# Quarter-array projections of a two-branch attention kernel: roundings, subtractions, no-operations and query loads placed by the planner, low parts written over their copies

## The chip, the cores and the metric

The kernel runs on one core of one Trainium2 chip. The metric is the device time of one execution in microseconds (us); the time given for a kernel is the median of several runs. A profiled execution adds a trace of what every engine did.

## The reference

Two attention blocks over the same input `x` (2048 rows of 448), each with its own weights, are mixed by a gate per row:

```
g = sigmoid((x * gate_w).sum(-1, keepdims=True))
a = A_ref(x, A_wqkv, A_wo)     # 16 heads of 28; each row attends to itself and 7 earlier rows, 2 apart
b = B_ref(x, B_wqkv, B_wo)     # 16 heads of 28; full softmax attention over all 2048 rows
return g * a + (1 - g) * b
```

Both blocks project `x` by a 448x1344 matrix to queries, keys and values and end with a 448x448 output product. All data is 32 bits wide.

## The kernel before, in words

**Two parts for one number.** A 32-bit operand is held as a rounded high part (type float32r) and a low part, the difference between the number and its high part. A product is the sum of three: high by high, high by low, low by high.

**Stages.** The kernel has (1) the first eleven projection tiles, which use all 128 rows of the TensorE array; (2) the quarter-array projections, which the change touches; (3) the attention of block B, 16 units of 16 steps, with block A's work on VectorE and GpSimd beside it; (4) the output products.

**Stage 2.** It makes tiles 11 to 90 of the list `tiles`: 17 tiles of queries and keys of B (512 columns), 16 of values of B and 47 of the 48 for A (448 columns; the last is made later by `last_tile`). Here every matmul uses 32 rows of the array, a quarter, and four run side by side. The function `quarters` (L391) writes the order of the matmuls out in advance. It keeps a planned time for TensorE, VectorE and ScalarE and for each of the eight PSUM banks, takes the matmul that can start first, and appends it to `plan`. A tile takes up to 42 quarter matmuls, all into one bank, first one quarter's share, then the next one's (`TURN`). Between two quarters of one tile stands a no-operation on GpSimd or ScalarE (L363): it waits for the last matmul of the one quarter, and the first of the other waits for it (the code's reason is "other rows, same bank"). An instruction on a queue waits for those ahead of it, a no-operation too.

**Score maxima.** Block B subtracts from its scores the maximum of each row. The maxima of the first 320 of 1024 score blocks are computed in stage 2, between the projections: `s1_quarter` (L169) issues one matmul of keys by queries (L152; one of four heads, so also a quarter of the array) into a free bank and one VectorE reduction of 512 columns out of it (L172). Sixty-four of them are a unit. `AHEAD` (L389) limits how many matmuls one head may be ahead of the one furthest behind. The queries of a unit lie in a pair of tiles, `QP[u % 2]`, so unit 2 uses the pair of unit 0. `load_qhi(u + 1)` (L150) is called when the first matmul of unit u is issued.

**Around a tile.** When the last matmul of a query or key tile is done, `qk_tile` (L464) copies the bank to SBUF on ScalarE (`raw`, L472), rounds the copy to the high part on ScalarE (`qkh`, L473) right behind it, has GpSimd subtract (L256) after 32 further product matmuls, and stores both parts to HBM after 43 (SP queue, L461). The three results take three half tiles of the pool `pp`, which has 16. Value and A tiles are only copied (L478). The weights of the next tiles are rounded on ScalarE (L324) and subtracted on GpSimd (L256). The maxima of a finished unit are gathered by `max_parts` (L182): a small VectorE reduction, two ScalarE instructions and one GpSimd subtraction (L193).

After stage 2 all eight banks are given back, and the attention begins with new PSUM tiles (`T`, `av`).

Of the kernel before, what the change touches and what calls it, by code (L numbers as in the profile page):

```python
# [21 lines left out]
NU = NG * NB  # L22
# [4 lines left out]
def gated_mix_kernel(ctx: ExitStack, tc: tile.TileContext, xT, xn, gw, wA, wB, woAB, out):  # L27
# [116 lines left out]
    def s1_mm(n, bank):  # L144
# [4 lines left out]
        if i == 0 and u + 1 < NU:  # L149
            load_qhi(u + 1)  # L150
        r = slice(32 * h, 32 * h + ROWS)
        nc.tensor.matmul(bank, qhis[u][h % 2][r, 128 * qs:128 * qs + 128],  # L152
                         KH[u // NB % 3][r, 512 * kc:512 * kc + 512], start=True, stop=True)
# [14 lines left out]

    def s1_quarter(h, bank):  # L169
        n = 4 * count[h] + h  # L170
        s1_mm(n, bank)
        nc.vector.tensor_reduce(MX[:, n % NMX:n % NMX + 1], bank, axis=X, op=ALU.max)  # L172
# [56 lines left out]
    if True:  # L229
# [10 lines left out]
        queue, sent = [], [0]  # L240
        clock = [0.0, 0.0, 0.0]

        def pool_op(cost, f):
            clock[1] = max(clock[1], clock[0]) + cost
            f()

        def soon(k, f):
            queue.append((sent[0] + k, f))
            queue.sort(key=lambda x: x[0])

        def run_queue():
            while queue and queue[0][0] <= sent[0]:
                queue.pop(0)[1]()

        def low_part(lo, raw, hi):
            soon(32, lambda: pool_op(0.3 + 0.002 * lo.shape[-1], lambda: nc.gpsimd.tensor_tensor(  # L256
                out=lo, in0=raw, in1=hi.bitcast(F32), op=ALU.subtract)))


        def both(dst, src, eng=nc.sync):  # L260
            for h in (0, 64):
# [53 lines left out]
        def split_w(wi, kts):  # L315
            if wi not in wsets:
                wsets[wi] = ([KL[0][:, 512 * i:512 * i + 512].rearrange("p (k c) -> p k c", k=4) for i in range(2)]
                             if wi == 2 else
                             [wp.tile([128, 4, 450], F32R, tag=g, name=f"{g}{wi}") for g in ("wh", "wl")])
            wh, wl = wsets[wi]  # L320
            r, t, n = wraw[wi]
            for kt in kts:
                raw = r[:, kt, :n] if kt < 3 else t[:, :n]
                nc.scalar.activation(wh[:, kt, :n], raw, AF.Copy)  # L324
                if wi > 1:
                    low_part(wl[:, kt, :n], raw, wh[:, kt, :n])
                else:
                    nc.gpsimd.tensor_tensor(out=wl[:, kt, :n], in0=raw, in1=wh[:, kt, :n].bitcast(F32), op=ALU.subtract)

# [6 lines left out]
                 for n in range(2)]  # L336

        SECOND = [(0, 0, 3), (0, 1, 3), (0, 0, 0), (0, 1, 0), (0, 0, 1), (0, 1, 1), (1, 0, 0), (0, 0, 2), (0, 1, 2),
                  (1, 0, 1), (1, 0, 2)]

        def product(n, p, q, bank, first, last, leaves=False):
            t = tiles[n]
            ws = wsets[t[0]]
            rows = slice(0, 128) if q is None else slice(32 * q, 32 * q + 32)
            a, c, k = p
            if t[1] == "qk":
                x = (xh[t[2]], xl[t[2]])[a][rows, k, :]
                i = nc.tensor.matmul(bank, ws[c][rows, k, t[4]:t[4] + 128], x, start=first, stop=last)  # L348
            else:
                j = t[-1]  # L350
                cols = D + 2 * (t[0] == GATE)
                x = (xh[j // 4], xl[j // 4])[a][rows, k, 128 * (j % 4):128 * (j % 4) + 128]
                i = nc.tensor.matmul(bank[:, 0:cols], x, ws[c][rows, k, 0:cols], start=first, stop=last)  # L353
            if q is not None:
                if n in moved:
                    follows(i, moved.pop(n))
                if leaves:
                    at_ = clock[0] + REACH
                    if max(clock[1], at_) <= max(clock[2], at_) + WORD:
                        eng, clock[1] = nc.gpsimd, max(clock[1], at_) + WORD  # L360
                    else:
                        eng = nc.scalar
                    moved[n] = eng.nop()  # L363
                    follows(moved[n], i)

        moved = {}
# [19 lines left out]

        TURN = ((0, 4, 3, 2, 1), (1, 0, 4, 3, 2), (2, 1, 0, 4, 3), (3, 2, 1, 0, 4))
        LOAD, REACH, SUM, NOP, WORD = 0.107, 0.43, 0.598, 0.16, 0.05
        HUNGER, AHEAD = 0.1, 2  # L389

        def quarters(n0, n1, maxima):  # L391
            todo = [[n for k in range(n0, n1, 5) for n in (k + i for i in TURN[q]) if n < n1] for q in range(4)]
# [6 lines left out]
            plan = []  # L399
            while any(todo) or any(stay):  # L400
                b = min(range(8), key=lambda i: free[i])

# [4 lines left out]
                for q in range(4):  # L407
# [11 lines left out]
                    if p[0] < 1e8 and (best is None or p < best):  # L419
                        best = p  # L420
                t, product_, q, wait = best
                issue, now_, begun[q] = max(issue, wait) + 0.003, t, t
                if not product_:
                    sent[q] += 1
                    end[q] = t + 0.2315
                    dve = max(dve, t + REACH) + SUM
                    free[b] = dve + 0.092 + WORD
                    plan.append((t, act, "max", q, b))
                    continue
                if not stay[q]:  # L430
                    n = todo[q].pop(0)
# [12 lines left out]
                plan.append((t, act, "product", n, p, q, home[n], first, last, leaves and not last))  # L444
# [6 lines left out]
            return plan  # L451


        fini = []
# [1 line left out]
        def qk_store(nb, rows, hi, lo):  # L456
            cs = slice(512 * nb, 512 * nb + 512)
            for dst, t in ((qk_hi, hi), (qk_lo, lo)):
                o = 0
                for r0, r1 in rows:  # L460
                    dma_r(dst[r0:r1, cs], t[o:o + r1 - r0])  # L461
                    o += r1 - r0

        def qk_tile(n, bank, now_, nb, rows):  # L464
            hi, lo = ptile("qkh").bitcast(F32R), ptile("qkl").bitcast(F32R)
            if n < FULL:
                nc.scalar.activation(hi, bank, AF.Copy)
# [3 lines left out]
            raw = ptile("raw")  # L471
            nc.scalar.activation(raw, bank, AF.Copy)  # L472
            nc.scalar.activation(hi, raw, AF.Copy)  # L473
            low_part(lo, raw, hi)
            soon(43, lambda: qk_store(nb, rows, hi, lo))

        def copy_tile(bank, dst):
            nc.scalar.activation(dst, bank[:, 0:D].rearrange("p (c e) -> p c e", e=dst.shape[-1]), AF.Copy)  # L478

        stage = {}  # L480

        def a_tile(n, bank, i, j):
            k = i, j // 2
            s = stage.get(k)
            if s is None:
                stage[k] = pair("ast").rearrange("p a b -> p (a b)")[:, 0:896].rearrange("p (c j e) -> p c j e", c=8, j=2)
            copy_tile(bank, stage[k][:, :, j % 2, :])
            if tiles[n][0] == GATE:
                nc.scalar.activation(zt[:, j:j + 1], bank[:, D:D + 1], AF.Copy)
            if s is not None:  # L490
                j -= j % 2
                nc.sync.dma_start(a_own[i][:, :, j:j + 2, :].rearrange("c p j e -> p c j e"), stage.pop(k))
# [93 lines left out]
        def behind(n):  # L586
# [12 lines left out]
                load_w(1, (True,))  # L599
            if n == 40:  # L600
                for i in range(4):
                    soon(20 * i, lambda i=i: init_kl(KL[0][:, 512 * i:512 * i + 512]))
            if n == 16:
                for i in (1, 2):
                    nc.sync.dma_start(a_scr[i][:, 0:NJ, :].rearrange("c j e -> c (j e)").rearrange(
                        "c (a b) -> c a b", b=NJ), omg[0:8, None, :].to_broadcast([8, 56, NJ]))
            if n == 32:
                for i in range(2):
                    soon(20 * i, lambda i=i: nc.gpsimd.memset(V[:, 8 * i:8 * i + 8, :, DH:], 1.0))
            if n == 22:  # L610
                load_k(1, KH[1], qk_hi)
            if n == 62:
# [7 lines left out]
            if n == 64:  # L620
                for sgn, dst in ((-1.0, g_t), (1.0, omg)):
                    e = sp.tile([128, NJ], F32, name="ez")
                    nc.scalar.activation(e, zt, AF.Exp, scale=sgn)
                    nc.gpsimd.tensor_tensor(out=e, in0=e, in1=V[:, 0, :, DH], op=ALU.add)
                    gate.append((dst, e))
            if n in (66, 68):
# [18 lines left out]
            behind(n)  # L645
        n = FULL
        before(n)
        for clock[0], clock[2], kind, *x in quarters(FULL, len(tiles) - 1, MAXIMA):
            if kind == "max":
                s1_quarter(x[0], PS[x[1]])  # L650
                continue
            product(*x[:3], PS[x[3]], *x[4:])
            sent[0] += 1
            run_queue()
# [6 lines left out]
        assert not queue  # L661

# [592 lines left out]
```

## Time and profile before

| | |
|---|---|
| median of 3 runs | 896.5 us (896.09 to 896.72) |
| the profiled execution's own time | 896.25 us |
| its span, first to last instruction | 894.5 us |
| quarter-array projections in it | about 36 to 249.4 us |
| attention and output products | 249.4 to 894.5 us |
| busy over the span: TensorE, VectorE, ScalarE, GpSimd | 881.3, 746.8, 610.1, 544.5 us |
| mean granted TensorE clock | 0.998 of full speed |

In the profile, PE is TensorE's matmuls and PEld its weight loads (each matmul has one), DVE is VectorE, ACT ScalarE, POOL GpSimd, SP the queue that issues DMAs. A "q" behind an engine (ACTq) means the queue's own instructions, such as the no-operations. "Idle before" is the time in which the engine did nothing before an instruction, and the name behind the arrow is what ended it. Matmuls overlap here, so PE counts as busy even when only one of four quarters works. Times are from the span's start.

### The profile page before, as it was taken

To read this page: it belongs to the slowest core of one execution; us is meant where nothing else is said; L and a number is where in the kernel's file an instruction comes from. 1 tells how busy PE (TensorE), PEld (TensorE's weight loads), DVE (VectorE), ACT (ScalarE), POOL (GpSimd) and SP (SyncE) were. 2 spreads that over 40 slices of the span, in tenths; PEclk is the share of its full clock that TensorE was granted. 3 is DMA by queue.
4 is the path that set the end of the run, shared out by engine and by line. 5 is a ranking of instruction groups with operands and counts; after the bars stand their busy time and mean duration, and the time that the engine had idled before them with its cause. 6 is when DMAs were issued, how large, how long until landed. Compare 5 with 4: busy or idle time off the path is not lost.

```text
span 894.5 us, 24181 instructions
## 1 busy us (share of the span) xinstructions
PE 881.3 (99%) x9988; PEld 525.9 (59%) x9988; DVE 746.8 (83%) x1128; ACT 610.1 (68%) x780; POOL 544.5 (61%) x413
## 2 busy tenths in 40 slices
PE   9997999999999999999999999999999999999998
PEld 7886999999954444444444444444444444434997
DVE  7685999999989999999999999999999999832221
ACT  6253223231178898898988989989889898897220
POOL 1164311020059689998989989999999799701000
PEclk9999999999999999999999999999999999999999
DMA  9868503445392251225225322433121321337691
GB/s 263 265 220 232 171 14 97 117 115 136 85 289 67 84 141 49 65 63 156 71 57 141 87 58 89 126 92 105 47 60 31 92 44 46 106 82 209 174 284 52
DMA packets 114199, 104.76 MB, mean 117 GB/s; under 512 B 75256, under 2 KB 82424, under 8 KB 113304
## 3 DMA queue, kind: packets, MB, share of 16 engines
q1 hardware_dynamic: 113656, 102.42, 41.0%
q8 instruction: 78, 1.28, 0.6%
q10 hardware_dynamic: 432, 0.79, 0.3%
q14 instruction: 33, 0.27, 0.1%
HBM read 62.20 MB, written 40.96 MB: 115 GB/s over the span
## 4 chain that ended last, share of the span: by engine, by line
PE 89%; DVE 1%; DMA 1%; ACT 0%; issue 0%; SPq 0%; POOLq 0%; ACTq 0%
PE T L1157 31%; PE av L1123 28%; PE r L353 14%; PE T L991 8%; PE T L152 4%; PE r L152 2%; PE r L348 2%; DVE MX L172 1%; DMA QP<-qk_hi 1%; PE av L553 0%; ACT P L1162 0%; SPq L104 0%; ACT onhi L1048 0%; ACT raw L472 0%; DVE res L1112 0%
## 5 line engine op out<-in xcount | busy, mean ns | idle before, releaser
L1162 ACT ACTIVATE P<-T 128x1024 f32<-128x1024 f32 x512 | 496.7, 1023 | 59.2 <-PE T L1157 57.4
L158 DVE TENSOR_REDUCE MX<-T 128x1 f32<-128x512 f32 x470 | 442.2, 954 | 31.7 <-PE T L152 20.2
L1123 PE MATMUL av<-P,V 128*32 128x512 f32 x2048 | 272.7, 605 | 0.0
L1157 PEld LDWEIGHTS T<-QH,KH 30*128 30x128 f32 x1024 | 92.3, 181 | 230.0 <-ACT P L1162 196.5
L152 PE MATMUL T<-KH,QP 30*128 30x512 f32 x704 | 220.9, 458 | 0.0
L1157 PE MATMUL T<-QH,KH 30*128 30x512 f32 x1024 | 211.9, 489 | 1.1 <-DVE MX L172 0.9
L172 DVE TENSOR_REDUCE MX<-r 128x1 f32<-128x512 f32 x320 | 197.1, 683 | 15.8 <-PE r L152 11.4
L1157 PE MATMUL T<-QH,KL 30*128 30x512 f32 x1024 | 185.5, 393 | 0.0
L1157 PE MATMUL T<-QL,KH 30*128 30x512 f32 x1024 | 183.2, 388 | 0.0
L353 PE MATMUL r<-wh,xh 32*128 32x448 f32 (+1 forms) x1008 | 150.8, 368 | 0.7 <-POOLq L363 0.7
L353 PE MATMUL r<-wl,xh 32*128 32x448 f32 (+1 forms) x882 | 144.4, 364 | 0.0
L758 POOL TENSOR_TENSOR prod<-qt,kt 128x896 f32<-128x896 f32 x64 | 135.5, 2118 | 3.3 <-DMA kt<-a_scr 3.3
L353 PE MATMUL r<-wh,xl 32*128 32x448 f32 (+1 forms) x756 | 136.3, 364 | 0.0
L353 PEld LDWEIGHTS r<-wh,xh 32*128 32x128 f32 x1008 | 125.6, 184 | 2.3 <-POOLq L363 1.5
L152 PE MATMUL r<-KH,QP 30*128 30x512 f32 x320 | 120.6, 404 | 5.4 <-DMA QP<-qk_hi 5.3
L353 PEld LDWEIGHTS r<-wl,xh 32*128 32x128 f32 x882 | 119.2, 185 | 0.1
L353 PEld LDWEIGHTS r<-wh,xl 32*128 32x128 f32 x756 | 107.0, 185 | 0.1
L819 POOL TENSOR_TENSOR oat<-oat,prod 128x896 f32<-128x896 f32 x48 | 101.3, 2110 | 2.0
L152 PEld LDWEIGHTS T<-KH,QP 30*128 30x128 f32 x704 | 86.0, 181 | 25.6 <-ACT P L1162 15.4
L814 POOL TENSOR_TENSOR prod<-vt,L 128x896 f32<-128x896 f32 x56 | 95.4, 1704 | 0.3
L1157 PEld LDWEIGHTS T<-QL,KH 30*128 30x128 f32 x1024 | 94.0, 184 | 0.0
L1157 PEld LDWEIGHTS T<-QH,KL 30*128 30x128 f32 x1024 | 92.9, 182 | 0.2
(134 smaller groups left out, 1057.8 us busy)
## 6 DMA issues: line engine op xcount, KB each, us to landing
a_scr<-ast SPq DMA_DIRECT2D x24, 448.0 KB
qk_hi<-qkh SPq DMA_DIRECT2D x24, 256.0 KB
qk_lo<-qkh SPq DMA_DIRECT2D x24, 256.0 KB
rbc<-rs SPq DMA_DIRECT2D x64, 64.0 KB
QP<-qk_hi SPq DMA_DIRECT2D x64, 56.0 KB
KL<-qk_lo SPq DMA_DIRECT2D x16, 224.0 KB
QH<-qk_hi SPq DMA_DIRECT2D x64, 56.0 KB
QL<-qk_lo SPq DMA_DIRECT2D x64, 56.0 KB
```

The costliest lines, as they stand in the source:

```text
L152: nc.tensor.matmul(bank, qhis[u][h % 2][r, 128 * qs:128 * qs + 128], KH[u // NB % 3][r, 512 * kc:512 * kc + 512], start=True, stop=True)
L158: i = nc.vector.tensor_reduce(MX[:, n % NMX:n % NMX + k], bank, axis=X, op=ALU.max)
L172: nc.vector.tensor_reduce(MX[:, n % NMX:n % NMX + 1], bank, axis=X, op=ALU.max)
L348: i = nc.tensor.matmul(bank, ws[c][rows, k, t[4]:t[4] + 128], x, start=first, stop=last)
L353: i = nc.tensor.matmul(bank[:, 0:cols], x, ws[c][rows, k, 0:cols], start=first, stop=last)
L758: nc.gpsimd.tensor_tensor(out=p, in0=qt[c], in1=kvt["k", c % 2][:, HALO - DIL * w:HALO - DIL * w + NJ, :], op=ALU.mult)
L814: nc.gpsimd.tensor_tensor(out=dst.rearrange("p j (h d) -> p j h d", d=DH), in0=kvt["v", c % 2][:, HALO - DIL * w:HALO - DIL * w + NJ, :].r ...
L819: nc.gpsimd.tensor_tensor(out=ows[c % 2][:, :, 0:56] if w == W - 1 else oat[c], in0=oat[c], in1=oat[c, w], op=ALU.add)
L991: writes(bank, nc.tensor.matmul(bank[:, cols], src, wo[c][k][:, cols], start=(first and k == ks[0] and i == 0), stop=(last and k == ks[-1] ...
L1123: nc.tensor.matmul(av[32 * h:32 * h + 32, :], V[:, kt, 4 * g + h, :], tiles_[h], start=(kt == 0), stop=(kt == NJ - 1), skip_group_check=True)
L1157: nc.tensor.matmul(bank[a], (KH[g % 3], KH[g % 3], KL[g % 2])[t][r, ks], (qh, ql, qh)[t][r, :], start=(t == 0), stop=(t == 2))
L1162: e = nc.scalar.activation(p, one if a == "2" else mine, AF.Exp, scale=SCALE).ins
```

## The change

- **Query loads.** `load_qhi(u + 1)` is no longer called at the first matmul of unit u, but when all four heads have issued their 64 of the unit before; the very first matmul still loads unit 1. `AHEAD` goes from 2 to 1.
- **Roundings.** The high part of a query or key tile is no longer rounded right behind its copy. The planner puts a "round" into the plan at the first time at which it sees ScalarE free, and plans the copy alone (0.607 in place of 1.214) ahead of the release of the bank.
- **Low parts.** The subtraction writes over the copy (`lo = raw`), so that a tile takes two half tiles and not three. Subtractions (of weights too) are taken from a list of jobs when they fit before the next no-operation; where a whole one does not fit, it is split into two halves of the columns. The stores follow the second half.
- **No-operations.** GpSimd or ScalarE is chosen by planned times of both, which now count the copies, roundings and subtractions that were placed.
- **Memsets and gate.** The memsets of `V` and `KL` and the gate's two additions go through the same list; the gate's two reciprocals come one tile later each.

```diff
     def s1_quarter(h, bank):
         n = 4 * count[h] + h
-        s1_mm(n, bank)
+        if n == 0:
+            load_qhi(1)
+        s1_mm(n, bank, True)
...
             if done % 64 == 0:
                 finished.append(done // 64 - 1)
+                if done < MAXIMA:
+                    load_qhi(done // 64 + 1)
...
+        def soon(delay, f, pool=(), patience=4.0):
+            jobs.append((clock["now"] + delay, clock["now"] + delay + patience, pool, f))
+            jobs.sort(key=lambda x: x[0])
...
+                if pool:
+                    begin = max(clock["pool"], t)
+                    room = turns[0] + 0.3 - begin if turns else 9.0
+                    fit = [c for c in pool if c <= room] or [c for c in pool[-1:] if t >= late]
+                    if begin > t + 0.1 or not fit:
+                        continue
...
+        def low_part(lo, raw, hi, delay, then=None):
...
+                nc.gpsimd.tensor_tensor(out=lo[:, p], in0=raw[:, p], in1=hi[:, p].bitcast(F32), op=ALU.subtract)
...
+            soon(delay, part, (1.28, 0.75))
...
-        HUNGER, AHEAD = 0.1, 2
+        HUNGER, AHEAD = 0.1, 1
...
+                if round_ and max(act, round_[0][0]) <= t:
+                    act = max(act, round_[0][0]) + 0.64
+                    plan.append((t, "round", round_.pop(0)[1]))
...
-                    act += 1.214 if cols[n] == 512 else 0.553
+                    act += 0.607 if cols[n] == 512 else 0.553
+                    if cols[n] == 512:
+                        round_.append((act + 0.1, n))
...
+        def qk_round(n):
+            _, _, nb, rows, _ = tiles[n]
+            hi, raw = ptile("qkh").bitcast(F32R), raws_.pop(n)
+            lo = raw.bitcast(F32R)
+            nc.scalar.activation(hi, raw, AF.Copy)
...
+            low_part(lo, raw, hi, 0.75, lambda: soon(0.9, lambda: qk_store(nb, rows, hi, lo)))
```

Three places show how the order moves. First, TensorE at the change from unit 0 to unit 1 of the maxima. The rows are matmuls, output<-inputs; L152 is a maximum's matmul, QP00 and QP01 hold the queries of unit 0 and later of unit 2, QP10 and QP11 those of unit 1. Before:

```order
L348 MATMUL r4_144<-xl1_208,KL0_169 128x512
L353 MATMUL r6_152<-wl3_927,xh0_203 128x448 [waits Pool_49]
L152 MATMUL r3_140<-KH0_167,QP01_174 128x512 [waits DMAHW2_49,Activation_49]
L348 MATMUL r5_148<-xl3_210,KL0_169 128x512
L353 MATMUL r2_136<-wh3_926,xh0_203 128x448 [waits DVE_49]
L353 MATMUL r6_152<-wh3_926,xl0_207 128x448
L353 MATMUL r0_128<-wl3_927,xh2_205 128x448
```

Now:

```order
L390 MATMUL r4_144<-wh3_908,xh0_203 128x448
L385 MATMUL r1_132<-xh3_206,KL0_169 128x512
L385 MATMUL r3_140<-xl2_209,KL0_169 128x512
L385 MATMUL r6_152<-xh1_204,KL0_169 128x512
L152 MATMUL r2_136<-KH0_167,QP00_173 128x512 [waits DVE_49]
```

In both, one head issues its last matmul of unit 0 after the others have begun unit 1. Before, the load of unit 2 into the same tile stood ahead of it in the program, so it waits for that load (DMAHW2); now the load stands behind it, and it waits for a bank alone.

Second, ScalarE at the second group of query and key tiles: a row from a bank (r0 to r7) is a copy, a row from `raw` or `qkr` a rounding. Before:

```order
L472 ACTIVATE raw_812<-r2_136 128x512
L473 ACTIVATE qkh_1061<-raw_812 128x512
L472 ACTIVATE raw_1079<-r7_156 128x512
L473 ACTIVATE qkh_1078<-raw_1079 128x512
L472 ACTIVATE raw_1079<-r1_132 128x512
L473 ACTIVATE qkh_1088<-raw_1079 128x512
L472 ACTIVATE raw_1102<-r6_152 128x512
```

Now:

```order
L522 ACTIVATE qkr_1044<-r5_148 128x512
L522 ACTIVATE qkr_1044<-r0_128 128x512
L522 ACTIVATE qkr_1086<-r1_132 128x512
L352 ACTIVATE wh3_908<-wt_606 128x448
L522 ACTIVATE qkr_1086<-r3_140 128x512
L522 ACTIVATE qkr_1103<-r2_136 128x512
L510 ACTIVATE qkr_1103<-qkr_1044 128x512
L510 ACTIVATE qkh_1163<-qkr_1044 128x512
```

Before, each copy waited behind the rounding of the tile ahead of it; now five copies stand ahead of the first rounding.

Third, GpSimd at the same place: subtractions of `qk` tiles and of the weights `wl`. Before:

```order
L256 TENSOR_TENSOR wl3_927<-raw_610,wh3_926 128x448 x3
L256 TENSOR_TENSOR qkh_1061<-raw_812,qkh_1061 128x512
L256 TENSOR_TENSOR qkh_1078<-raw_1079,qkh_1078 128x512
L256 TENSOR_TENSOR qkh_1088<-raw_1079,qkh_1088 128x512
L256 TENSOR_TENSOR qkh_1101<-raw_1102,qkh_1101 128x512
```

Now:

```order
L280 TENSOR_TENSOR wl3_909<-raw_605,wh3_908 128x448
L280 TENSOR_TENSOR qkr_785<-qkr_785,qkh_854 128x256 x2
L280 TENSOR_TENSOR wl3_909<-raw_605,wh3_908 128x224
L280 TENSOR_TENSOR wl3_909<-wt_606,wh3_908 128x224
L280 TENSOR_TENSOR wl3_909<-raw_605,wh3_908 128x224
L280 TENSOR_TENSOR qkr_1044<-qkr_1044,qkr_1103 128x256
```

Whole subtractions in a row have become halves, and halves of weights and of tiles alternate. The no-operations are not listed in these rows. Counted in the two programs, 198 stood on GpSimd and 42 on ScalarE before, 210 and 30 now; 15 of GpSimd's stood right behind a subtraction before, 34 now; and stage 2 has 37 subtractions before and 63 now. The 320 maxima and the quarter matmuls of the products are the same in number.

More of the change, by code (lines that the diff above doesn't have):

```diff
@@ L148, in s1_mm @@
             qs, kc = i // 8 % 4, 2 * (i // 32) + i // 4 % 2
-        if i == 0 and u + 1 < NU:
+        if i == 0 and not early and u + 1 < NU:
             load_qhi(u + 1)
@@ L238, in split @@
             nc.vector.tensor_tensor(out=lo, in0=raw, in1=hi.bitcast(F32), op=ALU.subtract)
[L240 to L257, printed above, removed]
+        jobs, sent, turns = [], [0], []
@@ new lines, in gated_mix_kernel, with run_jobs @@
+        clock = {"now": 0.0, "pool": 0.0, "act": 0.0}
+        def soon(delay, f, pool=(), patience=4.0):
+            jobs.append((clock["now"] + delay, clock["now"] + delay + patience, pool, f))
+            jobs.sort(key=lambda x: x[0])
+        def run_jobs(t):
+            clock["now"] = t
+            while turns and turns[0] < t:
+                turns.pop(0)
+            for j in list(jobs):
+                ready, late, pool, f = j
+                if ready > t:
+                    break
+                if pool:
[4 more added lines that the diff above has]
+                        continue
+                    clock["pool"] = begin + fit[0]
+                    jobs.remove(j)
+                    f(fit[0])
+                    continue
+                jobs.remove(j)
+                f()
@@ new lines, in act_busy, with part @@
+        def act_busy(cost, ready=0.0):
+            clock["act"] = max(clock["act"], clock["now"], ready) + cost
+        def low_part(lo, raw, hi, delay, then=None):
+            n = lo.shape[-1]
+            def part(c, begin=0):
+                p = slice(begin, n if c > 1 or begin else n // 2)
+                nc.gpsimd.tensor_tensor(out=lo[:, p], in0=raw[:, p], in1=hi[:, p].bitcast(F32), op=ALU.subtract)
+                if p.stop < n:
+                    soon(0.0, lambda c: part(c, p.stop), (0.75,), 2.0)
+                elif then:
+                    then()
+            soon(delay, part, (1.28, 0.75))
@@ L357, in product @@
                 if leaves:
[L358 to L363, printed above, removed]
+                    then = clock["now"] + REACH
+                    key = min(("pool", "act"), key=lambda k: max(clock[k], then) + WORD * (k == "act"))
+                    clock[key] = max(clock[key], then) + WORD
+                    moved[n] = (nc.gpsimd if key == "pool" else nc.scalar).nop()
                     follows(moved[n], i)
@@ L443, in quarters @@
                 last, leaves = not left[n], not stay[q]
-                plan.append((t, act, "product", n, p, q, home[n], first, last, leaves and not last))
+                plan.append((t, "product", n, p, q, home[n], first, last, leaves and not last))
                 if leaves:
@@ L470, in qk_tile @@
                 return
[L471 to L475, printed above, removed]
+            raws_[n] = ptile("qkr")
+            nc.scalar.activation(raws_[n], bank, AF.Copy)
+            act_busy(0.607, clock["now"] + REACH)
         def copy_tile(bank, dst):
             nc.scalar.activation(dst, bank[:, 0:D].rearrange("p (c e) -> p c e", e=dst.shape[-1]), AF.Copy)
+            act_busy(0.553, clock["now"] + REACH)
         stage = {}
@@ L647, in gated_mix_kernel @@
         before(n)
-        for clock[0], clock[2], kind, *x in quarters(FULL, len(tiles) - 1, MAXIMA):
+        plan = quarters(FULL, len(tiles) - 1, MAXIMA)
+        turns.extend(x[0] + REACH for x in plan if x[1] == "product" and x[8])
+        for t, kind, *x in plan:
+            run_jobs(t)
             if kind == "max":
@@ L660, in gated_mix_kernel @@
                 before(n)
-        assert not queue
+        assert not jobs
     hooks = {}
```

33 lines of the change are left out of this document (22 added, 11 removed).

## The prediction

> **What bounds the kernel now.** I read the mean times by stretch first: one row for the first part of the quarter-array stage, which holds nearly all its query and key tiles, one for the rest. Columns: stretch, length, busy time and count of PE, PEld, DVE, ACT and POOL, granted TensorE clock, DMA share, GB/s.
>
> ```profile
> 36.00:100.00 64.00, 56.73 (x904) 52.05 (x900) 50.41 (x83) 21.86 (x43) 25.09 (x24) 0.97 0.75 225
> 100.00:250.00 150.00, 148.41 (x2769) 145.56 (x2765) 147.09 (x249) 40.85 (x102) 20.02 (x25) 1.00 0.38 101
> ```
>
> From 100 us on TensorE and VectorE are both full (2765 weight loads in 150 us, 18.4 per us). Before 100 us both have holes: 52.05 of 64 us of weight loads, 50.41 of 64 us on VectorE. What the change can bring lies there. Next the waits of the weight loads from 36 to 250 us, since matmuls overlap and a weight load shows when the issue stands still (columns: total us, times, longest):
>
> ```profile
> PEld r L152 <- issue: 5.7, 1, 5.7
> PEld r L348 <- ACTq L363: 3.0, 3, 1.6
> PEld r L353 <- POOLq L363: 1.5, 2, 1.1
> PEld T L1157 <- DVE MX L172: 1.2, 1, 1.2
> PEld r L152 <- DVE MX L172: 0.8, 3, 0.3
> PEld r L348 <- POOLq L363: 0.3, 1, 0.3
> ```
>
> Together 12.5 us. The first is one stop of 5.7 us, the next three of ScalarE's no-operations. TensorE's timeline places them (start, length, row, idle time before it and what ended it):
>
> ```profile
> 53.61 0.50 PE L348 MATMUL r<-xh,wh 32*128 32x512 f32 x1 [0.70 <-ACTq L363]
> ...
> 69.17 0.49 PE L348 MATMUL r<-xh,wh 32*128 32x512 f32 x1 [1.21 <-ACTq L363]
> ...
> 87.16 0.76 PE L152 MATMUL r<-KH,QP 30*128 30x512 f32 x1 [5.33 <-DMA QP<-qk_hi]
> ...
> 173.06 0.47 PE L353 MATMUL r<-wh,xh 32*128 32x448 f32 x1 [0.72 <-POOLq L363]
> ```
>
> The long one is a maximum's matmul that waits for queries to land. VectorE's waits in the stage are the other side of these holes, 15.1 us in all:
>
> ```profile
> DVE MX L172 <- PE r L152: 11.4, 10, 6.6
> DVE MX L172 <- PE r L348: 2.5, 2, 2.3
> DVE MX L172 <- PE r L353: 1.2, 1, 1.2
> ```
>
> From 237.27 us to the stage's end the chain of work lies on VectorE (20 reductions), so it bounds the stage as closely as TensorE does:
>
> ```profile
> 237.27 12.12 DVE MX L172 x20
> ```
>
> **The change part by part.** *Query loads.* The SP queue issues the four loads of unit 2 here, and the clock's rows after the stop follow (stretch, PE busy, granted clock, DMA share, GB/s):
>
> ```profile
> 81.24 1.61 SPq L104 DMA_DIRECT2D QP<-qk_hi  x4
> ```
>
> ```profile
> 86.00:87.00 1.00, 0.00 (x0) 0.90 1.00 328
> 87.00:88.00 1.00, 0.84 (x8) 0.50 0.77 199
> 88.00:89.00 1.00, 1.00 (x14) 0.50 0.89 203
> 89.00:90.00 1.00, 1.00 (x18) 0.50 0.88 213
> 90.00:91.00 1.00, 1.00 (x23) 0.89 0.41 94
> ```
>
> The loads were issued when unit 1 began, and head 3 still had its last matmul of unit 0 to issue, out of a tile that one of them writes. It waited until they had landed, and all four quarters stood behind it. Now the load is issued after that matmul, and unit 2 is needed 64 maxima later, some 39 us at 0.61 us each (12.12 / 20). So the 5.7 us go whole. The clock at half speed behind the stop goes with them: 0.84 us of work and two whole rows at half, and a tenth of a row, 0.42 + 0.5 + 0.5 + 0.11, some 1.5 us. The Trainium skill (TensorE: Matmul & The Clock Gate, "What's actually happening") says that the clock drops to half after an idle window of about 3.4 us, for at least one such window; the rows agree. By its figure a whole window would have cost 1.7 us, and the sum below would be 0.2 us lower.
>
> SP now waits for the unit's last matmul before it issues the loads, and stores of the next tiles are queued behind it. I cost that at nothing: the half tiles those stores free are needed only after several more tiles. Without that cover it would cost one such group of issues, 1.6 us. A lower `AHEAD` gives the planner fewer choices for a maximum's head; since from the 64th on the maxima stand some 20 to 40 products earlier in TensorE's order than before (counted in the two orders), I cost it at nothing too.
>
> *Roundings.* ScalarE's share in the stage:
>
> ```profile
> L473 ACT ACTIVATE qkh<-raw 128x512 fp32r<-128x512 f32 x17 | 10.7, 632 | 0.9
> L472 ACT ACTIVATE raw<-r 128x512 f32<-128x512 f32 x17 | 9.9, 585 | 15.8 <-PE r L348 9.4 <-PE r L152 6.4
> ```
>
> The tiles come in groups of about five. Five pairs are 5 x 1.22 us, 6.1 us in one piece, and the no-operations at 53.61 and 69.17 us stood behind such pieces; the copies, which free banks, were spaced by roundings. Now five copies take 2.9 us, and the roundings follow. The two ACTq waits that the timeline shows go. The third, too short to show there, is of a no-operation behind the gathering of unit 0's maxima, which keeps its form; of the 3.0 us I leave 0.3 for it. So 2.7 us. What is late next at those places is a bank, held by VectorE, and that is work, no hole.
>
> *Subtractions and half tiles.* GpSimd's rows, by form:
>
> ```profile
> L256 POOL TENSOR_TENSOR qkh<-raw,qkh 128x512 fp32r<-128x512 f32 x17 | 21.4, 1287 | 15.6 <-ACT qkh L473 7.9 <-DMA qk_hi<-qkh 7.7
> L256 POOL TENSOR_TENSOR wl<-raw,wh 128x448 fp32r<-128x448 f32 x9 | 10.4, 1158 | 31.3 <-PE r L152 15.9 <-PE r L353 14.2 <-ACT wh L324 1.2
> L256 POOL TENSOR_TENSOR KL<-raw,KL 128x128 fp32r<-128x128 f32 x3 | 1.3, 446 | 13.0 <-PE r L348 13.0
> ```
>
> A half of 256 columns I estimate between the first and the last row: 446 + (1287 - 446) / 3 is 726 ns, so each split adds some 165 ns to GpSimd, 26 splits 4.3 us. GpSimd is busy 25 of the first 64 us; that is hidden as long as no no-operation waits behind it. The 7.7 us for a store to free a half tile go, since a tile takes two of 16 now; TensorE waited for none of it, so I count nothing.
>
> *No-operations.* One stood behind a gathering at 173 us:
>
> ```profile
> 173.02 0.22 POOL L193 TENSOR_TENSOR nmt<-nmv,nmt 128x16 fp32r<-128x16 f32 x1 [20.88 <-ACT nmv L192]
> ```
>
> The gatherings stay as they are, so I leave the POOLq waits of this kind in. Right behind a subtraction stood 15 of GpSimd's before, and 34 stand there now. The price is bounded by two rows: all 15 behind whole subtractions together cost at most the 0.3 us of the POOLq wait at L348 (the 1.5 us at L353 belong to another kind, no-operations behind a gathering's subtraction, below), so 19 more would cost 0.4 us; at the other end each waits for a whole half, 19 x 0.73, 13.9 us. Below nothing: the better choice of queue could also take the 1.8 us of POOLq waits. I take 0.9 us, near the row that shows the same thing.
>
> *The rest.* Memsets, the gate's additions and reciprocals are small, and their results are read in the attention, 40 us and more later; nothing. The attention and what follows (249.4 to 894.5 us) keep their order and 704 maxima, and move as one piece.
>
> The sum: 5.7 + 1.5 + 2.7 - 0.9 is 9.0 us off the profiled execution's own 896.25 us, 887.25 us. The median of the runs shown is 0.25 us higher, so I forecast 887.5 us. VectorE allows it, having 15.1 us of holes.
>
> **The rivals.** *Draining the banks is the bound (faster still).* If TensorE's smaller waits for banks, under 0.25 us and in no row above, vanish too because copies come earlier, the stage shrinks until VectorE's holes are gone: at most 15.1 us, or 12.2 if the 2.9 us remain that it is not busy after 100 us (150 - 147.09). That is 884.3 us, with 881.4 as the end. For it speaks the chain's end on VectorE; against it, that 18.4 weight loads per us are already reached between 100 and 250 us, and the sum of TensorE's holes is smaller. The Trainium skill (TensorEngine Tiling (Array Packing), "PSUM Bottleneck") has the rule that tiling speeds up the array but not the emptying of PSUM, which may become the bottleneck. The trace agrees in part: both are full.
>
> *Half of it comes back.* The plan is made of planned times; where a copy or rounding runs later than planned, subtractions and no-operations behind it do too. If each of the three groups of tiles keeps one hole of the size seen (1.2 or 1.6 us), or the gatherings cost 1.1 us four times in place of once, 3.3 (3 x 1.1) to 4.8 us (3 x 1.6) return: 890.8 to 892.3 us.
>
> *No-operations behind halves (slower).* Place: GpSimd's queue during the query and key tiles and at each weight set. If the 19 added ones wait 0.73 us each, 13.9 us against 9.9 gained: 4 us slower, 900.5 us. It turns slower at 0.52 us each. Against it speaks the 0.3 us for 15.
>
> *The change doesn't do what it says.* If another matmul still waits for a load, or a bank held by VectorE stands where the stop was, only the ScalarE part remains: 2.7 - 0.9, 894.7 us. Against it: the only late matmul of unit 0 now waits for a bank alone.
>
> **How the numbers follow.** Forecast 0.62 (its own range 885.5 to 890), the faster rival 0.12, half of it back 0.15, no-operations slower 0.06, the change without its main part 0.05. The range 883.5 to 893.5 us leaves out the slower rival, the last one and the tail of the faster. A difference of 0.2%, 1.8 us, is what a measurement of this kernel can tell from none. Faster: 0.62 + 0.12 + 0.15 less the forecast's own risk of a hole that I don't see, 0.87; within 0.2%: 0.05, mostly the change without its main part; slower: 0.08, the no-operations and that unseen hole.
>
> **What would show it.** Right: no wait of PE or PEld for a DMA of QP between 36 and 250 us; the clock at 1.00 in every row there; ACTq waits under 0.6 us; VectorE's waits down to 3 to 6 us; its last reduction out of a bank r at about 240 us; 645 us from there to the end, as before. Wrong: POOLq waits above 5 us in total (no-operations), a DMA in front of L152 (queries) or of a copy (half tiles), or clearly fewer weight loads between 36 and 100 us than the 17.3 per busy us of now (900 / 52.05) without any named wait, which would put the loss on banks.

## The result, and the profile after

| | before | after |
|---|---|---|
| median of 4 runs | 896.61 us (896.09 to 896.86) | 883.37 us (883.11 to 883.54) |
| ratio, 95% interval | | 0.9853 (0.9836 to 0.987) |
| the profiled execution's own time, its span | 896.25, 894.5 us | 883.11, 881.3 us |
| quarter-array projections end at | 249.4 us | 236.3 us |
| attention and output products | 645.1 us | 645.0 us |

The change makes the kernel 13.2 us faster. All of it comes out of the quarter-array stage, which ends 13.1 us earlier. The forecast was 887.5 us, a gain of 9.0 us, with 883.5 us as the low end, so the direction was right and the size too small.

The mean times by stretch of the kernel after, with the columns as before; the second stretch ends at 237 us now, just behind the end of the stage:

```profile
36.00:100.00 64.00, 64.00 (x1109) 62.51 (x1109) 63.19 (x105) 25.23 (x51) 34.00 (x49) 1.00 0.75 226
100.00:237.00 137.00, 136.72 (x2560) 133.75 (x2556) 134.96 (x228) 36.65 (x93) 15.47 (x27) 1.00 0.41 109
```

The first stretch, which was the one with holes, is full: 1109 weight loads where there were 900, VectorE busy 63.19 of 64 us where it was 50.41, the clock at 1.00. The second stretch has the density it had. The waits of the weight loads from 36 to 238 us:

```profile
PEld r L152 <- DVE MX L174: 0.7, 3, 0.3
PEld T L1212 <- ACT ast L526: 0.7, 1, 0.7
PEld r L390 <- ACT zt L538: 0.5, 2, 0.3
PEld r L390 <- POOLq L398: 0.4, 1, 0.4
PEld av L603 <- issue: 0.4, 1, 0.4
PEld r L385 <- DVE MX L174: 0.3, 1, 0.3
```

Together 3.0 us, where there were 12.5. The query stop is gone, no ACTq wait is left, and POOLq is down from 1.8 to 0.4 us. VectorE's waits in the same stretch, which were 15.1 us:

```profile
DVE MX L158 <- PE T L152: 1.2, 1, 1.2
DVE MX L174 <- PE r L152: 0.8, 3, 0.4
```

The end of the stage in the chain of waits (start, length, what):

```profile
232.39 1.04 PE r L390 x16
233.43 0.17 PE r L152
233.61 0.61 PE r L390 x11
...
234.25 0.66 PE r L390 x10
...
235.74 0.55 ACT ast L526
236.29 0.04 issue
236.33 0.50 PE T L1212 x2
```

Before, the last 12 us of the stage hung on VectorE's reductions; now its end hangs on TensorE's product matmuls and the last copy. From 36 to 237 us the rows above leave VectorE idle for 2.9 of 201 us and the weight loads for 4.7, so little is left to gain in this stage by moving work about.

### The profile page after: what moved, and what is told of

Same layout as the page of the kernel before. It is cut to its first block, busy times and chain, and to the rows that moved or that the text cites. A ratio compares the mean times of both kernels' runs of the same rounds, so it can differ in the third digit from the quotient of the medians.

```text
span 881.3 us, 24193 instructions
## 1 busy us (share of the span) xinstructions
PE 876.9 (100%) x9988; PEld 524.6 (60%) x9988; DVE 747.3 (85%) x1128; ACT 609.3 (69%) x780; POOL 549.1 (62%) x439
## 4 chain that ended last, share of the span: by engine, by line
PE 99%; ACT 0%; issue 0%; DVE 0%; ACTq 0%
PE T L1212 31%; PE av L1178 29%; PE r L390 15%; PE r L385 8%; PE T L1046 8%; PE T L152 4%; PE r L152 3%; PE r L227 1%; PE av L603 0%; ACT P L1217 0%; ACT ast L526 0%; ACT onhi L1103 0%; DVE res L1167 0%; ACT L L839 0%; ACTq L1103 0%
## 5 line engine op out<-in xcount | busy, mean ns | idle before, releaser
L152 PE MATMUL T<-KH,QP 30*128 30x512 f32 x704 | 220.7, 458 | 0.0
L390 PE MATMUL r<-wl,xh 32*128 32x448 f32 (+1 forms) x882 | 146.6, 363 | 0.0
L390 PE MATMUL r<-wh,xl 32*128 32x448 f32 (+1 forms) x756 | 139.8, 362 | 0.0
L390 PEld LDWEIGHTS r<-wh,xh 32*128 32x128 f32 x1008 | 129.9, 184 | 1.3 <-ACT zt L538 0.5
L152 PE MATMUL r<-KH,QP 30*128 30x512 f32 x320 | 123.3, 400 | 0.0
L390 PEld LDWEIGHTS r<-wl,xh 32*128 32x128 f32 x882 | 121.0, 184 | 0.1
L390 PEld LDWEIGHTS r<-wh,xl 32*128 32x128 f32 x756 | 110.9, 184 | 0.1
L152 PEld LDWEIGHTS T<-KH,QP 30*128 30x128 f32 x704 | 86.0, 181 | 25.9 <-ACT P L1217 16.3
```

## The experiments

Four theories stand in the expectations. **S**: the gain is a sum of the stops that the trace of before names (query load, no-operations on ScalarE and GpSimd). **V**: it ends where VectorE has no holes left. **B**: what the sum lacks are small waits for banks whose copies stand behind roundings. **P**: it is TensorE's new order. Unless said otherwise a kernel keeps the order of TensorE's instructions of the kernel that it is made from. The kernel before ran beside each: its median was 897.03, 896.94 and 897.02 us in the three groups, 0.4 us above that of the table, so differences under half a microsecond between groups are not told apart.

**The late query load alone, on the kernel before.**

```diff
-    def s1_mm(n, bank):
+    def s1_mm(n, bank, early=False):
...
-        if i == 0 and u + 1 < NU:
+        if i == 0 and not early and u + 1 < NU:
             load_qhi(u + 1)
...
-        s1_mm(n, bank)
+        if n == 0:
+            load_qhi(1)
+        s1_mm(n, bank, True)
...
             if done % 64 == 0:
                 finished.append(done // 64 - 1)
+                if done < MAXIMA:
+                    load_qhi(done // 64 + 1)
```

> The kernel before with one part of the change: the queries of unit u+1 are loaded when all four heads have issued the last matmul of unit u-1's tile pair, not at unit u's first matmul; the order of TensorE is that of before. Theory S (each named stop is a term of its own): 5.7 us of stop and 1.5 us of half clock go, 7.2 us in all, 889.4 us. Theory V (VectorE bounds the stage, so a stop of TensorE costs only what VectorE was starved): its 6.63 + 1.21 us of idle there go, 888.8 us. If the stop was covered by the VectorE queue at the stage's end, less than 4 us: over 892.5 us.

Measured: 890.08 us (889.85 to 890.28), ratio 0.992 (0.9905 to 0.9935), 6.95 us less than before. The waits of its weight loads from 36 to 236 us:

```profile
PEld r L352 <- ACTq L367: 4.1, 4, 1.6
PEld r L357 <- POOLq L367: 1.4, 2, 1.1
PEld r L152 <- DVE MX L174: 0.6, 2, 0.3
PEld r L352 <- POOLq L367: 0.3, 1, 0.3
```

and TensorE's timeline at the three largest of the first row:

```profile
53.64 0.50 PE L352 MATMUL r<-xh,wh 32*128 32x512 f32 x1 [0.70 <-ACTq L367]
...
69.20 0.49 PE L352 MATMUL r<-xh,wh 32*128 32x512 f32 x1 [1.20 <-ACTq L367]
...
83.59 0.50 PE L352 MATMUL r<-xh,KL 32*128 32x512 f32 x1 [0.72 <-ACTq L367]
```

The load's term, 7.2 us in the forecast, holds. The third row is new: a no-operation of ScalarE at 83.59 us, which in the kernel before fell, as I read it, into the query stop (about 82 to 87 us) and so did not show: ScalarE's copies and roundings from 78 to 84 us stand at the same places there. ACTq waits are 4.1 us once that stop is gone, not 3.0.

**The query load back at the unit's first matmul, in the kernel after.**

```diff
-        if n == 0:
-            load_qhi(1)
-        s1_mm(n, bank, True)
+        s1_mm(n, bank)
...
-                if done < MAXIMA:
-                    load_qhi(done // 64 + 1)
```

> The changed kernel with the query load put back to the first matmul of the unit; all else and the order of TensorE as changed. Theory S: the stop comes back with its clock, 883.4 + 7.2 = 890.6 us, and a wait of PE for a DMA of QP near the change from unit 0 to 1. Theory V: the same or a little more, 891 us. Where the load lands faster than before because the SP queue is less full at that moment, the stop is 2 to 3 us and the clock stays full: 885.5 to 886.5 us.

Measured: 893.51 us (892.35 to 894.08), ratio 0.9957 (0.9942 to 0.9972), 10 us more than the kernel after. TensorE's timeline has three stops where the kernel before has one:

```profile
81.82 0.76 PE L152 MATMUL r<-KH,QP 30*128 30x512 f32 x1 [4.36 <-DMA QP<-qk_hi]
...
123.03 0.47 PE L152 MATMUL r<-KH,QP 30*128 30x512 f32 x1 [1.13 <-DMA QP<-qk_hi]
...
205.16 0.46 PE L152 MATMUL r<-KH,QP 30*128 30x512 f32 x1 [1.46 <-DMA QP<-qk_hi]
```

Its clock around the first (stretch, busy time of five engines, clock, DMA share, GB/s):

```profile
80.00:81.00 1.00, 0.00 (x0) 0.00 (x0) 0.00 (x0) 0.00 (x0) 0.00 (x0) 0.53 0.97 346
...
85.00:86.00 1.00, 1.00 (x17) 1.00 (x14) 0.77 (x2) 0.20 (x2) 0.00 (x0) 0.50 1.01 365
86.00:87.00 1.00, 1.00 (x17) 1.00 (x14) 0.69 (x1) 1.00 (x4) 0.80 (x2) 0.55 1.09 291
...
123.00:124.00 1.00, 0.97 (x20) 0.95 (x24) 0.47 (x1) 0.00 (x0) 0.00 (x0) 1.00 0.12 41
```

The stops are 7.0 us (4.36 + 1.13 + 1.46), and half speed from the restart at 81.8 to 86.9 us costs 2.5 more; that is 9.5 of the 10 us. In the new order a head is late at three changes of unit, so loads issued at a unit's first matmul cost more there than in the old order. The place of the load is worth 7 us in the old order and 10 in the new.

**Each rounding right behind its copy, in the kernel after.**

```diff
-                    if cols[n] == 512:
-                        round_.append((act + 0.1, n))
...
             nc.scalar.activation(raw, bank, AF.Copy)
+            qk_round(n)
```

> The changed kernel with every rounding right behind its copy again, the order of TensorE kept. Theory S: the two ACTq stops come back, 2.7 us, 886.1 us. Theory B (the 4 us that the forecast lacked were small waits for banks held by a late copy): those come back as well, 6 us or more, 889 us or slower, with fewer weight loads between 50 and 75 us (429 matmuls there now, 375 before). Theory P (the gain beyond the stops lies in the new order of TensorE): 884 to 886 us, since the order is kept.

Measured: 888.86 us (888.5 to 889.12), ratio 0.9906 (0.989 to 0.9923), 5.5 us more than the kernel after. The weight loads wait for copies that stand behind roundings:

```profile
PEld r L152 <- ACT qkr L520: 3.2, 6, 1.0
PEld r L385 <- ACT qkr L520: 1.3, 2, 0.9
PEld r L390 <- ACT qkr L520: 1.2, 3, 0.6
...
PEld r L152 <- ACT V L525: 0.6, 1, 0.6
```

These 6.3 us are what theory B names: many waits of at most 1 us for a bank that ScalarE has yet to copy. None of these rows stands in the kernel after, and none in the kernel before or in the run with the late load alone. TensorE's order here is one that was planned for early copies; how much of the 5.5 us comes from its not fitting late ones is not shown, since no run has the order of before with the roundings placed by the plan.

**A half tile of its own for the low part, in the kernel after** (three half tiles for a tile, as before).

```diff
-            lo = raw.bitcast(F32R)
+            lo = ptile("qkl").bitcast(F32R)
```

> The changed kernel with low parts in a half tile of their own again, three per tile in place of two; order of TensorE kept. Theory S: the wait for a store to free a half tile was no stop of TensorE, so 883.4 us, within 0.5. If half tiles hold the copies back: a wait of ScalarE's copies for a DMA of qk_hi or qk_lo, and 885 to 890 us.

Measured: 886.61 us (886.41 to 888.36), ratio 0.9888 (0.9873 to 0.9902), 3.2 us more than the kernel after. Its longest wait of weight loads is

```profile
PEld r L385 <- ACTq L398: 3.2, 1, 3.2
```

and on TensorE's timeline the stop ends at 74.09 us:

```profile
74.09 0.49 PE L385 MATMUL r<-xh,KL 32*128 32x512 f32 x1 [2.81 <-ACTq L398]
```

ScalarE's timeline before it:

```profile
64.07 1.07 ACT L522 ACTIVATE qkr<-r 128x512 f32<-128x512 f32 x2
65.02 0.64 ACT L510 ACTIVATE qkh<-qkl 128x512 fp32r<-128x512 f32 x1
65.55 0.64 ACT L510 ACTIVATE qkh<-qkr 128x512 fp32r<-128x512 f32 x1
66.71 1.15 ACT L510 ACTIVATE qkh<-qkr 128x512 fp32r<-128x512 f32 x2 [0.53 <-DMA qk_hi<-qkl]
74.00 0.64 ACT L510 ACTIVATE qkh<-qkr 128x512 fp32r<-128x512 f32 x1 [6.14 <-DMA qk_hi<-qkl]
```

The fifth rounding of the group waits for a store to land before it starts. ScalarE stands still for 6.14 us, a no-operation stands behind the rounding in its queue, and TensorE stands behind the no-operation. In the kernel after the same place reads

```profile
63.73 1.08 ACT L522 ACTIVATE qkr<-r 128x512 f32<-128x512 f32 x2
64.69 0.64 ACT L510 ACTIVATE qkr<-qkr 128x512 fp32r<-128x512 f32 x1
65.21 2.20 ACT L510 ACTIVATE qkh<-qkr 128x512 fp32r<-128x512 f32 x4
```

five roundings in one piece.

**Both: rounding behind its copy, and three half tiles.** The two edits above in one kernel.

> The kernel after with the rounding right behind its copy and with a half tile of its own for the low part, TensorE's order as in the kernel after. Alone these cost 5.5 and 3.2 us. If they are two separate costs (banks held by late copies; ScalarE stopped by a half tile that a store frees): 891.5 to 892.8 us, and a stop of TensorE near 74 us with an ACTq name beside the waits of L152 for ACT copies. If they share their time (the roundings spaced by copies ask for half tiles later, so that the store is done): 888 to 890 us and no such stop; 890.1 is what the late load alone gave on the order of before.

Measured: 889.09 us (888.79 to 889.58), ratio 0.991 (0.9895 to 0.9925), within 0.3 us of the run with roundings behind alone. So the third half tile costs 3.2 us where roundings come from the plan, and nothing where they follow their copies. The rows that put this to the test are a copy of ScalarE and the last product matmuls of TensorE before it:

```profile
92.74 0.60 ACT L520 ACTIVATE qkl<-r 128x512 f32<-128x512 f32 x1 [8.13 <-DMA qk_hi<-qkr]
```

```profile
92.24 0.46 PE L385 MATMUL r<-xl,KL 32*128 32x512 f32 x2
```

The copy is put down to a store, with 8.13 us of idle time before it, but the last two product matmuls, one of which fills the bank that it reads, start from 92.24 us and end by 92.70, just before the copy starts. So this is no stop for a half tile, and ScalarE has no other wait for a store from 36 to 240 us, where the run with three half tiles alone has its 6.14 us. Why the half tiles suffice in this order of ScalarE's work and not in that of the plan is not shown.

**The late load and the low part over its copy, on the kernel before.** The first experiment with `lo = raw` in `qk_tile`.

> The kernel before with the late query load and with the low part written over its copy, TensorE's order as before, roundings still right behind the copies. The late load alone gave 890.1 us. If the half tiles cost anything in the order of before: 887 to 889 us. If their price exists only where the plan sends five roundings in a row (as the wait of the rounding for a store in the run with three half tiles suggests): 889.6 to 890.6 us, with the three ACTq waits of 1.0 to 1.6 us still there.

Measured: 890.03 us (889.88 to 890.09), ratio 0.992 (0.9903 to 0.9936), against 890.08 for the load alone. Its ACTq waits stay:

```profile
PEld r L352 <- ACTq L367: 4.0, 4, 1.6
```

In the order of before the low part's place is worth nothing, as the forecast said of it.

**Four edits of the kernel after that take back one part each.** Subtractions never split; `AHEAD` 2 (TensorE's order differs); all no-operations on GpSimd; each subtraction whole and at once behind its rounding:

```diff
-            soon(delay, part, (1.28, 0.75))
+            soon(delay, part, (1.28,))
```

> The changed kernel without halves: a subtraction is issued whole or waits until it may be late; order of TensorE kept. Theory S: a no-operation behind a subtraction costs little (0.3 us for 15 before), so 883.4 to 884.3 us. If no-operations do wait for the subtraction ahead of them, 19 or more of them by up to 1.28 us less 0.73: 885 to 893 us, with POOLq waits to match.

```diff
-        HUNGER, AHEAD = 0.1, 1
+        HUNGER, AHEAD = 0.1, 2
```

> The changed kernel with AHEAD 2, the load still after all four heads; the planner makes another order of TensorE. Theory S: no stop hangs on it once the load is moved, 883.4 us within 1. If the lower AHEAD itself brings part of the gain (heads closer together, fewer gatherings late), 884.5 to 887 us.

```diff
-                    key = min(("pool", "act"), key=lambda k: max(clock[k], then) + WORD * (k == "act"))
+                    key = "pool"
```

> The changed kernel with all no-operations on GpSimd; order of TensorE kept. Theory S: the choice of queue is worth at most the 30 on ScalarE, each waiting behind a subtraction for part of 0.73 us: 883.4 to 886 us, with POOLq waits at the places of the 30. If the choice of queue is what brought POOLq from 1.8 to 0.4 us, 885 us or slower.

```diff
-            soon(delay, part, (1.28, 0.75))
+            clock["pool"] = max(clock["pool"], clock["now"]) + 1.28
+            part(1.28)
```

> The changed kernel with each subtraction issued whole and at once behind its rounding, not fitted between no-operations; order of TensorE kept. Theory S (no-operations behind subtractions cost little): 883.4 to 885 us. If fitting them between the no-operations matters: POOLq waits of some 5 us and more, 888 us or slower, as the subtractions now wait at the head of the queue for the rounding, up to 1 us each for 33 of them.

| edit | median | ratio (95%) |
|---|---|---|
| never split | 883.1 us (883.05 to 883.29) | 0.9843 (0.9828 to 0.9857) |
| `AHEAD` 2 | 883.6 us (883.4 to 883.68) | 0.9849 (0.9835 to 0.9864) |
| no-operations on GpSimd | 883.26 us (882.81 to 883.66) | 0.9848 (0.9831 to 0.9864) |
| subtractions at once | 883.48 us (883.22 to 883.7) | 0.9848 (0.9834 to 0.9863) |

None differs from the kernel after by more than 0.3 us. Halves, their fitting between no-operations, the choice of the queue and `AHEAD` are each worth nothing measurable while the rest stands.

**Three of them at once.** `AHEAD` 2, subtractions at once, no-operations on GpSimd; what stays of the change are the load, the roundings and the low parts, besides the memsets and the gate.

> The kernel after with three things given back at once: AHEAD 2, each subtraction issued whole right behind its rounding, all no-operations on GpSimd. What is left of the change are the late query load, the roundings placed by the plan and the low parts over their copies. If these three are the whole gain (theory S with the ACT term corrected): 882.5 to 884.5 us, no wait of a weight load above 1 us between 36 and 236. If the parts without a price of their own cover for each other (each was taken back alone, with the others left in): POOLq waits of 2 us or more come back, 886 us or more.

Measured: 884.1 us (883.7 to 884.35), ratio 0.9854 (0.9839 to 0.9868). Its longest row of no-operation waits:

```profile
PEld r L391 <- POOLq L399: 0.9, 3, 0.4
```

So what stays makes 12.9 us (897.02 - 884.1), and the three parts that were taken back some 0.7 together. Of the theories, P falls as the main cause: TensorE's order of the kernel after gives 893.5, 888.9 or 886.6 us where one other part is taken back, and another order (`AHEAD` 2) gives 883.6. S gives the larger share; B is shown in the new order of TensorE only; V holds of the end, where VectorE has 2.0 us of waits left.

## Why the prediction was right in direction and too small in size

The runs make a path from before to after, with the terms of the sum beside its steps (medians, us):

| step | from, to | measured | forecast |
|---|---|---|---|
| late query load | 897.03, 890.08 | -6.95 | -7.2 |
| new orders, subtractions, no-operations | 890.08, 889.09 | -1.0 | +0.9 |
| roundings by the plan and low part over its copy, together | 889.09, 883.37 | -5.7 | -2.7 |
| sum | | -13.7 | -9.0 |

(The path starts from the 897.03 of the experiments' group; by the table's own 896.61 it is 13.2.) The third row has two parts, and its split hangs on which comes first: by way of 886.61 us the roundings are worth 2.5 and the low part 3.2; by way of 888.86 us the low part is worth 0.2 and the roundings 5.5. So no term can be blamed by the path alone. The waits that are gone say more. What is left to gain once the load is moved stands in the trace of the first experiment. Its stretch from 36 us to its last product matmuls, and the same of the kernel after:

```profile
36.00:242.50 206.50, 203.13 (x3656) 196.25 (x3648) 196.44 (x330) 61.80 (x141) 45.14 (x49) 1.00 0.50 141
36.00:236.00 200.00, 200.00 (x3652) 195.73 (x3648) 198.14 (x331) 61.16 (x142) 49.47 (x75) 1.00 0.52 146
```

The same 3648 weight loads stand still for 10.3 us in the one (206.50 - 196.25) and 4.3 us in the other. In the first experiment 6.4 us of it have a row (above: 4.1 for ScalarE's no-operations, 1.7 for GpSimd's, 0.6 for VectorE), in the kernel after 1.9 (0.4 for GpSimd's no-operations, 1.0 for VectorE, 0.5 for a small copy of ScalarE). So 4.1 us of ScalarE's no-operations are gone, 1.3 of GpSimd's, and 1.5 of waits too short for a row (3.9 to 2.4); 0.9 are new. That is 6.0 of the 6.7 us between the two kernels, where the forecast had 2.7 - 0.9, 1.8 us.

- **Query loads: right.** Stop and half clock were 7.2 us, and 6.95 came by the medians, 6.1 by the profiled executions (896.25 and 890.16 us); the executions of the kernel before behind the medians ran at a mean granted clock of 0.996, the profiled one at 0.998. That SP's wait would cost nothing held as well.
- **No-operations: the step that failed most, wrong in sign.** I charged 0.9 us for 19 more of GpSimd's no-operations behind subtractions, and left 1.8 us of POOLq waits in. No charge shows, and the waits fell from 1.7 to 0.4 us: 2.2 us off. The slower rival, 13.9 us for the same place, has nothing left. What took the waits is open: the runs with never-split or at-once subtractions, with `AHEAD` 2 and with all no-operations on GpSimd each keep the time of the kernel after, with POOLq waits of 0.3 to 0.4 us. Whether a no-operation does not wait or its wait is covered, these runs do not tell.
- **Roundings: mis-sized.** I took 2.7 us from no-operations behind rows of copies and roundings; 4.1 us of such waits are gone. The row I took it from was short by a stop that lay inside the query stop (83.59 us), and the 0.3 us that I left in went too. I also held that what is late next is a bank, "held by VectorE, and that is work, no hole". With roundings behind their copies in the new order no ACTq wait shows at all, and yet 5.5 us are lost, to banks that ScalarE has yet to copy.
- **Half tiles: nothing gained over before, as counted, but from a wait that was misread, and with a price that I did not see.** The 7.7 us "for a store to free a half tile" are no such wait. These are the rounding and the subtraction of that tile in the kernel before:

```profile
78.76 0.63 ACT L473 ACTIVATE qkh<-raw 128x512 fp32r<-128x512 f32 x1
79.53 6.20 POOL L256 TENSOR_TENSOR qkh<-raw,qkh 128x512 fp32r<-128x512 f32 x5 [7.70 <-DMA qk_hi<-qkh]
```

  The subtraction reads what the rounding ends writing at 79.39 us, so the store can have held it for 0.14 us at most. On the order of before the edit gives 0.05 us, and with roundings behind their copies 0.2. But the change does both at once: with the roundings placed by the plan and three half tiles to a tile, ScalarE waits 6.14 us for a store, with a no-operation and TensorE behind it, and 3.2 us are lost. The low part over its copy keeps that cost from coming up; I did not look for it.
- **The half subtractions' own duration was sized rightly.** From 36 to 237 us this group stands in GpSimd's rows, 740 ns against my 726:

```profile
L280 POOL TENSOR_TENSOR qkr<-qkr,qkh 128x256 fp32r<-128x256 f32 x20 | 14.5, 740 | 6.8 <-DMA qk_lo<-qkr 3.8 <-PE r L385 1.7 <-PE r L390 0.9
```

- **The faster rival: its figure came, its mechanism only in a small part.** It gave 884.3 us by VectorE's holes closing, with 881.4 as its end, and they closed from 15.1 to 2.0 us. But its reason was waits for banks under 0.25 us, and of waits too short for a row only 1.5 us went; more of what the forecast lacked were no-operations' waits that have rows. That its figure is so near is in part luck. I gave it 0.12 because the sum of TensorE's holes was smaller; the waits of up to 1 us for banks that ScalarE has yet to copy, in the run with roundings behind copies, have no row in the trace of before.
- **Half of it comes back, and the change without its main part: neither came.**

What stays open is the split of the 1.0 us in the second row among TensorE's new order, the queues of the no-operations and the time of the subtractions, and 0.7 us of the 6.7 that stand in no row.

## What to carry to other kernels

The waits that a profile names are not all there are: a long stop hides those that fall into it, so look what the other engines do during the stop before you leave their term small. When a wait is put down to a store, look when the other input was ready: the 7.7 and 8.13 us here ended within 0.2 us of a rounding and a matmul. Price two edits that share buffers together, because the one may make the wait that the other takes away: the half tile here is worth 0 us or 3.2 according to where the roundings stand. In this kernel it paid to let the queue that others wait on do first what frees a shared resource (the copies), and the roundings when it was free.

## What the runs showed of the hardware

- In the profiled executions TensorE ran at half speed after its longer stops and not after the shorter ones. After 4.36 us (the run with the load back) and 5.33 us (before) it did; after 2.81 (three half tiles, granted clock 1.00 from 73 to 78 us), 1.13 and 1.46 us it did not. The half speed lasted 3.4 us in the kernel before, by its clock rows, and 6.8 us in the run with the load back (0.94 + 5 + 0.9 of the rows from 80 to 87), twice as long after the shorter stop. The Trainium skill (TensorE: Matmul & The Clock Gate, "What's actually happening") gives a free-running window of about 3.4 us; both lengths agree with one and two of it.
- Executions of one kernel differ in this. With three half tiles one of four took 888.36 us at a mean granted clock of 0.998, the others 886.41 to 886.64 us at 1.0; half speed for 3.4 us would cost 1.7 us, an estimate from the length above, and the difference is 1.7 to 2.0. With the load back one took 892.35 us at 0.998, the others 893.12 to 894.08 us at 0.996. So the length of the stop does not settle how long the half speed lasts, and the first of these executions may have had one after its stop; without a trace of it that is not shown.
- Where GpSimd's no-operations stand among subtractions made no measurable difference in these kernels: counted in the programs, 16 (subtractions at once), 28 (never split), 39 (after) and 54 (all on GpSimd) stand right behind a two-input operation, and the medians lie between 883.1 and 883.5 us without a trend.
